# The first mixing written in two parts: weight conversions and one unit's scans beside the first channel products, the rest of three attention units beside what follows

## The chip, the cores and the metric

The program runs on one core of a Trainium2 chip. The metric is device time in microseconds (us) of one execution, from three runs of the kernel before: 521.94, 522.8 and 524.35, so a median of 522.8. A trace of another execution is shown below; its own time was 521.84 us.

## The reference

Two blocks follow each other. The first is a linear attention with a decaying state, for 4 batches, 8 heads, 768 positions and 48 features a head:

```
for t in range(S):
    cur = einsum('bhd,bhe->bhde', u * k[t], v[t])
    y[t] = einsum('bhd,bhde->bhe', r[t], state + cur)
    state = w[t][..., None] * state + einsum('bhd,bhe->bhde', k[t], v[t])
```

Its output, reshaped to x of 768 positions by 384 features a batch, goes into a mixer:

```
h = relu(x.T @ w_tok1) @ w_tok2        # tokens: 768 -> 256 -> 768
u = x + h.T
out = u + relu(u @ w_ch1) @ w_ch2      # channels: 384 -> 1536 -> 384
```

All of it is float32. The four mixer weights come in as 64-bit floats and are turned into float32 on the chip.

## The kernel before, in words

Attention is cut into 12 units: three for each of the four batches, each of 256 positions (two pieces of 128) and all 8 heads. `unit(i)` (L346) gives the steps of one unit as small functions:

- `ends` (L367): a backward scan of the decays on VectorE (L372), with a memset and a reciprocal. `keys` (L375) multiplies k by it (L377). `begins` (L379) is a forward scan (L380), `queries` (L382) multiplies r by that (L383).
- `tokens` and `copied`: TensorE transposes of the scaled keys into two PSUM banks (L287), ScalarE copies (L288).
- `own_u` (L385, ScalarE), `own_gram` (L390, TensorE) and `own_put` (L393, VectorE): the diagonal term with u. Units 0 to 3 make it this way; later units take it from an extra array `near` by VectorE (`products`, L397, and `sums_put`, L408).
- `gram` (L418) and `mask` (L421): products within a chunk of 64 positions and their masking.
- `carry` (L427): the outer products of keys and values. Then the chain over the four chunks of a unit: `update` (L440, VectorE, L448) adds to the state, `scaled` (L433, ScalarE, four small L438) scales it for the next chunk. Each `scaled` needs the `update` before it and each `update` the `scaled` before it.
- `before` (L450, TensorE L317): queries times the scaled states, so it needs the last `scaled`. `after` (L458, L338) adds the products within chunks, and `taken` (L462) copies the result into x.
- `ranges` (L361): two ScalarE passes (L364) that only flag decays out of range.

The mixing of a batch takes its x: `hidden` (L519) and `back` (L526) are the token part, `turn` (L533) transposes, then for each third of 256 positions come the channel products. In the first batch they are `up` (L540: six L545 matmul records for one of 12 column groups, then a ScalarE relu, L547) and `down` (L615: L621, twelve column groups summed in a PSUM bank, then a VectorE addition L625 and a store). The third third of the first batch uses `quarters` (L628, L639 and L643).

A weight is converted in pieces by `convert` (L195). A conversion loads one megabyte (two SP-queue transfers, L206) and runs on VectorE L209, L215, L221, L224 and twice L227, with L212 and L218 on ScalarE between L209 and L224. Two raw buffers alternate. Nine conversions, numbered 0 to 8 here, make up w_ch1 and w_ch2: 0 to 3 and half of 4 are w_ch1, the rest w_ch2. Conversions 0 and 1 are done before the channel products begin.

The order of the instructions on TensorE, VectorE and ScalarE is written out by hand: `strict` (L88) keeps each engine in the order in which the pieces are emitted. `woven` (L46) merges lists in proportion to costs given by hand: each piece has a cost, and pieces of two lists are sorted by the middle of their share of their list. Transfers on the SP queue are placed by the tile framework from the same order.

In the first batch (L820 to L828) three things are merged: the channel products of batch 0 (`ups`, `downs`), conversions 2 to 8, and all the steps of units 3, 4 and 5, which are batch 1's attention. `steps(i)` (L705) lists the steps of a unit, L828 weaves the three lists of steps over the whole stage. PSUM gives this stage six banks of one pool, which channel products, transposes and attention products share, and two banks for the outer products. Each later batch has its own order (`middle_mixing`, L800, and `last_mixing`, L778).

Of the kernel before, what the change touches and what calls it, by code (L numbers as in the profile page):

```python
# [24 lines left out]
UB = C // UC  # L25
# [20 lines left out]
def woven(*lists):  # L46

    keyed = []
    for n, pieces in enumerate(lists):
        total, at = sum(c for c, _ in pieces), 0.0  # L50
        for i, (c, f) in enumerate(pieces):
            keyed.append(((at + c / 2) / total, n, i, c, f))
            at += c
    return [(c, f) for *_, c, f in sorted(keyed, key=lambda e: e[:3])]
# [8 lines left out]
def rwkv6_then_mixer(  # L63
# [18 lines left out]
    pe, dve, act, pool, sp = nc.tensor, nc.vector, nc.scalar, nc.gpsimd, nc.sync  # L82
# [5 lines left out]
    def strict(*fs):  # L88

        for f in fs:  # L90
            done = len(block.instructions)
            f()
            for ins in block.instructions[done:]:
                if ins.engine in in_turn:
                    if in_turn[ins.engine]:
                        tc.add_manual_dep(ins, in_turn[ins.engine], no_sync, reason="order of issue")
                    in_turn[ins.engine] = ins.name
# [20 lines left out]
    u_rows = const.tile([128, DM], f32, name="u_rows")  # L118
# [10 lines left out]
    def load_w(i):  # L129
        if i < NU:  # L130
            for cols in (slice(MID, WCOLS), slice(0, MID)) if i == 0 else (slice(0, WCOLS),):
                sp.dma_start(ws[i % 2][:, cols], w[i][:, cols])

    def rk_of(i):
        return rks[i if i < UB else (i - UB) % 2]

    def load_rk(i):
        if i < NU:
            for n in (1, 0):
                for rows in (slice(0, 128),) if i < 3 else (slice(0, D), slice(P, P + D)):  # L140
                    sp.dma_start(rk_of(i)[rows, ts(n, COLS)], rk[i, n, rows, :])
# [3 lines left out]
    def load_v(i):  # L145
        if i < NU:
            vs[i] = vpool.tile([128, UC, DM], f32, name="vt")
            b, j = divmod(i, UB)
            sp.dma_start(vs[i], v[b, ts(j, UC * 128), :].rearrange("(c p) e -> p c e", p=128))

    def load_near(i):
        if UB < i < NU:
            nears[i] = apool.tile([128, UC, 2, DM], f32, name="near", bufs=1)
            sp.dma_start(nears[i], near[i - UB - 1])
# [82 lines left out]
    def conversion(*weights, rooms):  # L237
        pieces = [e for w in weights for e in blocks(*w)]
        return [convert(pieces[2 * n:2 * n + 2], *rooms(n)) for n in range(len(pieces) // 2)]
# [243 lines left out]
    def weight_sums(n):  # L483
        t1, t2, t4 = w_sums
        to, a, b = ((t1, w12, w11), (t2, w22, t1), (t4, w21, t2), (w12, w22, w12))[n]
        dve.tensor_sub(to, a, b)
# [11 lines left out]
    def less(to, a, b):  # L498
        dve.scalar_tensor_tensor(to, a, -1.0, b, op0=ALU.mult, op1=ALU.subtract)

    def left_sums():
        a = by_three
        return [lambda: dve.tensor_sub(A9, a(0, 1), a(1, 0)), lambda: dve.tensor_sub(A8, a(1, 0), a(1, 1)),
                lambda: dve.tensor_add(A0, a(1, 2), a(2, 1)), lambda: dve.tensor_add(A0, A0, A8), lambda: dve.tensor_sub(A8, A0, a(2, 1)),
                lambda: dve.tensor_sub(A7, a(0, 1), a(0, 0)), lambda: dve.tensor_sub(A12, a(2, 0), a(0, 2)),
                lambda: dve.tensor_add(A12, A12, A7), lambda: less(A11, A12, a(2, 2)), lambda: less(A7, A12, a(0, 2))]

    def lefts_in_place():
        a = by_three
        return [lambda: dve.tensor_sub(s_, A12, a(2, 0)), lambda: dve.tensor_sub(A2, A0, a(1, 2)),  # L510
                lambda: dve.tensor_sub(A10, a(1, 2), A9), lambda: dve.tensor_sub(A6, a(2, 2), A0), lambda: dve.tensor_sub(A13, a(0, 2), A9)]
# [190 lines left out]
    def mixing_of(bt):  # L702
        return mixing(bt, lambda: xs[bt], lambda n: out[bt, ts(n, 128), :])

    def steps(i):  # L705

        e = unit(i)
        up, by = e["updates"], e["scaled"]
        by_tokens = i > UB
        sums = e["products"] if by_tokens else [lambda: None] * 3  # L710
        some = lambda fs, c: [(c, f) for f in fs]
        return [(0.1, lambda: (i > UB and load_rk(i + 1), load_v(i + 1))), *([] if by_tokens else some(e["own_u"], 0.2)),
                (2.4, e["ends"]), (1.2, e["keys"]), (0.4, e["ranges"][0]), (2.2, e["begins"]), (1.0, e["tokens"]), (0.2, e["copied"][0]),
                *([] if by_tokens else [(1.0, e["own_gram"]), (1.3, e["own_put"]), (0.1, lambda: sp.dma_start(u_rows, u_all))]), (0.2, e["copied"][1]), (1.2, e["queries"]), (0.3, by[0]),
                (1.0, sums[0]), (1.0, e["carry"]), (1.0, sums[1]),
                (0.7, up[0]), (0.3, by[1]), (1.4, e["gram"]), (1.0, sums[2]), (0.1, lambda: load_near(i + 1)),
                (0.7, up[1]), (0.3, by[2]), (1.2, e["mask"]), (0.7, up[2]), (0.3, by[3]),
                *([(1.3, e["sums_put"])] if by_tokens else []), (0.7, up[3]),
                (0.1, lambda: load_w(i + 2)), (1.0, e["before"]), (0.1, e["seen"]), (1.5, e["ranges"][1]), (1.0, e["after"]), *some(e["taken"], 0.3)]
# [15 lines left out]
    hiddens, turned, ups, downs = mixing_of(0)  # L735
    h = [f for pair in zip(*hiddens) for _, f in pair]
    to_tok = conversion((wtok1, w_tok1, 2, 256), (wtok2, w_tok2, 2, 256), rooms=lambda n: (n % 2, n % 2))
    to_ch = conversion((wch1, w_ch1, 1, 512), (wch2, w_ch2, 4, 128), rooms=lambda n: (n % 2, 0) if n else (2, 1))
# [5 lines left out]
    e0, e1, e2 = (unit(i) for i in range(UB))  # L744
# [19 lines left out]
    def single(steps, n):  # L764
        return [(0.1, f) for f in (steps[5:] if n == 0 else steps[n < 3:])]
# [34 lines left out]
    def middle_mixing(bt):  # L800
        hiddens, turned, rights, thirds, quarters = mixing_of(bt)
        n = (bt + 1) * UB
        (a0, a1, a2), (b0, b1, b2), (c0, c1, c2) = (parts_of(i) for i in range(n, n + UB))
        *turned, end = turned
        of, sums = rights(0)
        hiddens = [e for h in hiddens for e in h]
        if bt == 1:
            a1[-5:-5] = products_of(n)
        pieces = woven(hiddens + turned[:6] + sums[:3] + turned[6:8] + sums[3:6] + turned[8:10] + sums[6:] + turned[10:], a0 + a1 + a2 + b0)
        for s, (att, near) in enumerate(((b1, n + 1), (b2 + c0, n + 2), (c1 + c2, n + 3))):  # L810
            ups = thirds(s, of)
            if s == 0:
                ups.insert(2, (0.01, end[1]))
            of, sums = rights(s + 1) if s < 2 else (None, [])
            pieces += ups[:1] + woven(ups[1:11], products_of(near) + sums[:2]) + ups[11:] + woven(att, woven(quarters(s), sums[2:]) if s < 2 else quarters(s))
        return pieces

    for bt in range(B):
        ahead = []
        if bt == 0:  # L820
            to_ch = [single(e, n) for n, e in enumerate(to_ch)]
            both = [f for e in zip(ups[0], ups[1]) for f in e]
            ahead = woven(turned, sum(to_ch[:2], []), [(1.3, e1["ranges"][1])])
            of_weights = [(0.1, lambda n=n: weight_sums(n)) for n in range(4)]
            both = woven(both[:6], [(1.3, f) for f in e2["ranges"]]) + both[6:]
            pieces = woven(both, sum(to_ch[2:8], [])) + woven(downs[0][:6], to_ch[8]) + downs[0][6:] + downs[1][:4]
            pieces += woven(downs[1][4:] + ups[2], of_weights + [(0.1, f) for f in left_sums()]) + woven(downs[2], [(0.1, f) for f in lefts_in_place()])
            pieces = woven([e for i in range(UB, 2 * UB) for e in steps(i)], pieces)  # L828
        elif bt < B - 1:
            pieces = middle_mixing(bt)  # L830
        else:
            pieces = last_mixing()
        strict(*(f for _, f in ahead + pieces))
# [113 lines left out]
```

## Time and profile before

| | |
|---|---|
| median of three runs | 522.8 us (521.94 to 524.35) |
| the profiled execution, its own time | 521.84 us |
| its span, first to last instruction | 520.1 us |
| TensorE, VectorE, ScalarE busy | 95%, 75%, 44% of the span |
| mean granted TensorE clock | 0.984 |

The first batch's channel products start at 63.71 us of the span and the token products of batch 1 (L522) at 179.66 us. By stages, with the busy time of each engine:

| stretch of the span, us | what | TensorE | VectorE | ScalarE | granted clock |
|---|---|---|---|---|---|
| 53.67 to 63.71 | `back` and `turn` of batch 0 | 9.51 | 7.76 | 6.86 | 1.00 |
| 63.71 to 79.90 | first channel products | 13.13 | 15.86 | 12.09 | 0.89 |
| 79.90 to 119.90 | up products, first down products | 39.84 | 33.66 | 25.35 | 1.00 |
| 119.90 to 179.66 | rest of batch 0 | 59.76 | 41.74 | 19.58 | 1.00 |
| 179.66 to 520.10 | batches 1 to 3 | 334.83 | 240.58 | 129.03 | 1.00 |

A float32 matmul shows as two records, so that one `up` group has six. The ends of matmuls are modelled, so a busy TensorE may be waiting inside; the distance from one start to the next tells more. Instructions on VectorE and ScalarE overlap the next one by about 0.1 us, and here too starts are compared.

### The profile page before, as it was taken

To read this page: it belongs to the slowest core of one execution; us is meant where nothing else is said; L and a number is where in the kernel's file an instruction comes from. 1 tells how busy PE (TensorE), PEld (TensorE's weight loads), DVE (VectorE), ACT (ScalarE), POOL (GpSimd) and SP (SyncE) were. 2 spreads that over 40 slices of the span, in tenths; PEclk is the share of its full clock that TensorE was granted. 3 is DMA by queue.
4 is the path that set the end of the run, shared out by engine and by line. 5 is a ranking of instruction groups with operands and counts; after the bars stand their busy time and mean duration, and the time that the engine had idled before them with its cause. 6 is when DMAs were issued, how large, how long until landed. Compare 5 with 4: busy or idle time off the path is not lost.

```text
span 520.1 us, 13317 instructions
## 1 busy us (share of the span) xinstructions
PE 492.2 (95%) x5794; PEld 429.4 (83%) x5794; DVE 388.1 (75%) x633; ACT 229.7 (44%) x533; POOL 1.3 (0%) x10
## 2 busy tenths in 40 slices
PE   3589979999999999999999999999999999999996
PEld 3476568866689868999999867999999859999996
DVE  7999798786596878987869668986858615684653
ACT  3868785671243236524335436524435414531300
POOL 0000000000000000000000000000000000000000
PEclk9779989999999999999999999999999999999999
DMA  8887448523314333122211432100000000000000
GB/s 305 320 262 208 135 145 279 168 89 115 104 38 133 92 112 84 62 69 66 63 62 62 142 96 63 61 18 15 3 32 1 18 15 1 1 2 33 0 33 33
DMA packets 20945, 46.06 MB, mean 89 GB/s; under 512 B 2128, under 2 KB 13008, under 8 KB 20880
## 3 DMA queue, kind: packets, MB, share of 16 engines
q1 hardware_dynamic: 20736, 45.14, 27.2%
q8 instruction: 47, 0.77, 0.6%
q14 instruction: 18, 0.15, 0.1%
q10 hardware_dynamic: 144, 0.00, 0.0%
HBM read 40.41 MB, written 4.72 MB: 87 GB/s over the span
## 4 chain that ended last, share of the span: by engine, by line
PE 76%; DVE 15%; ACT 5%; issue 3%; DMA 1%; DVEq 0%
PE z_ps L582 18%; PE q_ps L643 12%; PE q_ps L639 12%; PE z_ps L545 8%; PE h_ps L529 6%; PE h_ps L522 6%; PE h_ps L621 4%; PE gram L257 2%; PE y_ps L317 2%; PE y_ps L338 2%; DVE w L380 2%; PE xT_ps L537 2%; DVE z L590 2%; DVE to_end L372 1%; DVE rk L383 1%
## 5 line engine op out<-in xcount | busy, mean ns | idle before, releaser
L438 ACT ACTIVATE before<-state,to_end 112x48 f32<-112x48 f32 x176 | 44.4, 324 | 60.0 <-DVE state L448 56.5
L587 ACT COPY z<-z_ps 128x512 f32<-128x512 f32 x54 | 30.6, 587 | 57.4 <-PE z_ps L582 39.5
L590 DVE TENSOR_TENSOR z<-z,z_ps 128x512 f32<-128x512 f32 x54 | 35.9, 682 | 24.6 <-PE z_ps L582 15.9
L545 PE MATMUL z_ps<-xT,wch 128*128 128x256 f32 x216 | 50.1, 387 | 0.0
L599 ACT ACTIVATE z<-z 128x512 f32<-128x512 f32 x54 | 33.3, 631 | 33.1 <-DVE z L590 29.0
L545 PEld LDWEIGHTS z_ps<-xT,wch 128*128 128x128 f32 x216 | 40.8, 193 | 6.2 <-DVE wch L227 0.3
L639 PE MATMUL q_ps<-wch,z 128*128 128x192 f32 x222 | 42.9, 329 | 0.2
L643 PE MATMUL q_ps<-wch,z 128*128 128x192 f32 x222 | 43.0, 330 | 0.0
L639 PEld LDWEIGHTS q_ps<-wch,z 128*128 128x128 f32 x222 | 36.4, 190 | 0.9 <-ACT z L599 0.6
L643 PEld LDWEIGHTS q_ps<-wch,z 128*128 128x128 f32 x222 | 36.7, 190 | 0.5
L529 PE MATMUL h_ps<-h,wtok 128*128 128x384 f32 x96 | 35.1, 492 | 0.6 <-ACT h L524 0.6
L593 DVE TENSOR_TENSOR z<-z,z_ps 128x512 f32<-128x512 f32 x45 | 30.0, 683 | 7.0 <-PE z_ps L582 6.5
L522 PE MATMUL h_ps<-x,wtok 128*128 128x384 f32 x96 | 32.9, 490 | 0.0
L531 DVE TENSOR_TENSOR x<-x,h_ps 128x384 f32<-128x384 f32 x24 | 13.2, 552 | 26.2 <-PE h_ps L529 26.2
L621 PE MATMUL h_ps<-wch,z 128*128 128x384 f32 x96 | 32.4, 490 | 0.2 <-DVE wch L227 0.2
L582 PE MATMUL z_ps<-rk,wch 128*128 128x128 f32 x256 | 31.2, 275 | 0.0
L582 PEld LDWEIGHTS z_ps<-rk,wch 128*128 128x128 f32 x256 | 30.0, 192 | 0.0
L372 DVE TENSOR_TENSOR_SCAN to_end<-w,starts 112x1041 f32<-112x1041 f32 (+1 forms) x13 | 28.1, 2160 | 2.1 <-DMA w<-in_w_dram 1.7
L380 DVE TENSOR_TENSOR_SCAN w<-w,starts 112x1041 f32<-112x1041 f32 x12 | 27.8, 2320 | 0.0
L643 PE MATMUL q_ps<-scratch,z 128*128 128x192 f32 x144 | 27.9, 330 | 0.0
L621 PEld LDWEIGHTS h_ps<-wch,z 128*128 128x128 f32 x96 | 17.8, 190 | 11.6 <-DVE wch L227 0.3
L639 PE MATMUL q_ps<-scratch,z 128*128 128x192 f32 x144 | 27.3, 326 | 0.0
(181 smaller groups left out, 916.2 us busy)
## 6 DMA issues: line engine op xcount, KB each, us to landing
rk<-in_rk_dram SPq DMA_DIRECT2D x36, 192.0 KB, 3.8
near<-in_near_dram SPq DMA_DIRECT2D x8, 768.0 KB, 4.6
w<-in_w_dram SPq DMA_DIRECT2D x11, 520.5 KB, 4.7
vt<-in_v_dram SPq DMA_DIRECT2D x12, 384.0 KB, 3.7
out_dram<-o SPq DMA_DIRECT2D x24, 192.0 KB, 1.9
spare<-in_w_ch_dram SPq DMA_DIRECT2D x8, 512.0 KB, 4.5
scratch<-in_w_ch_dram SPq DMA_DIRECT2D x8, 512.0 KB, 5.2
rk<-in_rk_dram SPq DMA_DIRECT2D x6, 512.0 KB, 8.5
```

The source lines that it names most:

```text
L372: dve.tensor_tensor_scan(to, of, start, 0.0, op0=ALU.mult, op1=ALU.add)
L380: dve.tensor_tensor_scan(w_[:ROWS], w_[:ROWS], starts[:ROWS], 0.0, op0=ALU.mult, op1=ALU.add)
L438: act.mul(t[:ROWS, a], state[bt, g][:ROWS, a], by_last(c, j)[:, a:a + 1])
L522: pe.matmul(sums[i], wtok1[:, c, ts(i, 128)], x_of()[:, c, :], start=(c == 0), stop=(c == C - 1))
L529: pe.matmul(ps, wtok2[:, i, ts(c, 128)], h1[:, i, :], start=(i == 0), stop=(i == DTOK // 128 - 1))
L545: pe.matmul(ps, wch1[:, m, ts(jt, 128)], xT[:, m, ts(s, SEG)], start=(m == 0), stop=(m == DM // 128 - 1))
L582: pe.matmul(ps[:, q], lefts[r][:, ts(q, 128)], of[r], start=first and q == 0, stop=end and q == JB - 1, skip_group_check=True)
L590: dve.tensor_add(to(n), to(n), ps)
L599: act.activation(to(n), to(n), AF.Relu)
L621: pe.matmul(ps, zs[s][:, jt, ts(n, 128)], wch2[:, jt, :], start=(jt == 0), stop=(jt == NJ - 1))
L639: pe.matmul(L["q"], a[:, j, :], b[:, j, :], start=(j == 0), stop=False)
L643: pe.matmul(L["q"], a[:, j, :], b[:, j, :], start=False, stop=(j == HJ - 1))
```

## The change

`steps(i)` returns a unit in two lists, `first` (scans and what prepares the keys) and `second`. Unit 3's `first` is woven with conversions 2 to 8, all 24 `up` groups of the first two thirds and the first four `down` pieces. The rest of unit 3, all of units 4 and 5, and unit 2's two range flags are woven with the remaining products. Within unit 3, `own_gram`, `own_put`, the load of `u_rows`, the first range flag and `queries` move from between the scans into the second list. No instruction is added or removed, and the arithmetic stays.

```
@@ steps(i), at the end @@
-        return [(0.1, lambda: (i > UB and load_rk(i + 1), load_v(i + 1))), *([] if by_tokens else some(e["own_u"], 0.2)),
-                (2.4, e["ends"]), (1.2, e["keys"]), (0.4, e["ranges"][0]), (2.2, e["begins"]), (1.0, e["tokens"]), (0.2, e["copied"][0]),
-                *([] if by_tokens else [(1.0, e["own_gram"]), (1.3, e["own_put"]), (0.1, lambda: sp.dma_start(u_rows, u_all))]), (0.2, e["copied"][1]), (1.2, e["queries"]), (0.3, by[0]),
+        loads, ranges, copied = (0.1, lambda: (i > UB and load_rk(i + 1), load_v(i + 1))), (0.4, e["ranges"][0]), some(e["copied"], 0.2)
+        ends, keys, begins, tokens, queries = ((c, e[n]) for c, n in ((2.4, "ends"), (1.2, "keys"), (2.2, "begins"), (1.0, "tokens"), (1.2, "queries")))
+        if by_tokens:
+            first = [loads, ends, keys, ranges, begins, tokens, *copied, queries]
+        else:
+            first = [loads, *some(e["own_u"], 0.2), ends, keys, begins, tokens, *copied]
+        second = [] if by_tokens else [(1.0, e["own_gram"]), (1.3, e["own_put"]), (0.1, lambda: sp.dma_start(u_rows, u_all)), ranges, queries]
+        return first, [*second, (0.3, by[0]),
                 (1.0, sums[0]), (1.0, e["carry"]), (1.0, sums[1]),
...
@@ the order of batch 0 @@
-            both = woven(both[:6], [(1.3, f) for f in e2["ranges"]]) + both[6:]
-            pieces = woven(both, sum(to_ch[2:8], [])) + woven(downs[0][:6], to_ch[8]) + downs[0][6:] + downs[1][:4]
-            pieces += woven(downs[1][4:] + ups[2], of_weights + [(0.1, f) for f in left_sums()]) + woven(downs[2], [(0.1, f) for f in lefts_in_place()])
-            pieces = woven([e for i in range(UB, 2 * UB) for e in steps(i)], pieces)
+            (first, second), *rest = (steps(i) for i in range(UB, 2 * UB))
+            pieces = woven(first, woven(both, sum(to_ch[2:8], [])) + woven(downs[0][:4], to_ch[8]))
+            mixed = downs[0][4:] + downs[1][:4] + woven(downs[1][4:] + ups[2], of_weights + [(0.1, f) for f in left_sums()])
+            mixed += woven(downs[2], [(0.1, f) for f in lefts_in_place()])
+            pieces += woven([(0.4, f) for f in e2["ranges"]] + second + sum((a + b for a, b in rest), []), mixed)
```

## The prediction

> **What bounds the kernel now.** First the page's busy shares and clock row, then stage windows, then TensorE's timeline of the stage that the change reorders.
>
> ```profile
> PE 492.2 (95%) x5794; PEld 429.4 (83%) x5794; DVE 388.1 (75%) x633; ACT 229.7 (44%) x533; POOL 1.3 (0%) x10
> ...
> PEclk9779989999999999999999999999999999999999
> ```
> ```profile
> 63.71:79.90 16.19, 13.13 (x116) 10.94 (x115) 15.86 (x21) 12.09 (x22) 0.00 (x0) 0.89 0.44 135
> ...
> 119.90:179.66 59.76, 59.76 (x660) 47.12 (x661) 41.74 (x60) 19.58 (x59) 0.00 (x0) 1.00 0.30 91
> 179.66:520.10 340.44, 334.83 (x3558) 306.10 (x3556) 240.58 (x430) 129.03 (x295) 0.00 (x0) 1.00 0.15 45
> ```
>
> TensorE is the bound. From 63.71 us on it lacks work only in 63.71 to 79.90 (13.13 of 16.19 us busy, clock 0.89) and at the very end. The columns after the length are TensorE, weight loads, VectorE, ScalarE, GpSimd, then clock. Now the hole itself, on the timeline of TensorE and VectorE, and the clock in a window of 2 us:
>
> ```profile
> 63.71 6.82 PE L545 MATMUL z_ps<-xT,wch 128*128 128x256 f32 x30
> ...
> 72.27 1.22 DVE L377 TENSOR_TENSOR rk<-rk,to_end 112x1024 f32<-112x1024 f32 x1
> ...
> 73.59 1.94 PE L287 MATMUL k_ps<-ident,rk 128*128 128x128 f32 x8 [3.06 <-issue]
> ...
> 75.32 2.24 PE L545 MATMUL z_ps<-xT,wch 128*128 128x256 f32 x6
> ...
> 77.50 1.16 PE L257 MATMUL gram<-rk,near 48*64 48x64 f32 x64
> ```
> ```profile
> 74.00:76.00 2.00, 2.00 (x10) 0.50 0.39 138
> ```
>
> After five `up` groups TensorE reaches unit 3's transposes, whose keys (L377) VectorE writes only until 73.5. The trace calls the wait "issue"; the transposes read what L377 writes, so it is the keys. Thirty records at 0.2167 us end at 70.21, so 3.3 us are lost to 73.59. Then the clock reads 0.50: the eight transposes take 1.73 us to the next start (0.90 at 112.44), and six L545 take 2.18 against 1.30 plus 0.18 of switching. That adds 0.8 and 0.7. With 0.3 us of small waits (states at 98.18, a weight at 119.90), 5.1 us of this stage are recoverable.
>
> [...]
>
> **The change, first part.** 24 groups at 1.30 us come before any attention on TensorE, so the 3.3 + 1.5 us hole goes: the transposes stand behind them and one `down` piece, at 63.71 + 31.2 + 1.3 = 96.2, and the keys are long done. What can be late instead is the weights. On VectorE seven conversions and unit 3's scans must pass. The price of a conversion comes from these rows of the timeline, VectorE's and ScalarE's:
>
> ```profile
> 81.09 0.68 DVE L209 TENSOR_SCALAR scratch<-scratch 128x1024 uint16<-128x1024 uint16 x1
> ...
> 83.43 1.22 DVE L221 SCALAR_TENSOR_TENSOR scratch<-scratch 128x1024 f32<-128x1024 uint32 x1
> 85.53 0.69 DVE L224 TENSOR_TENSOR scratch<-scratch 128x1024 bf16<-128x1024 bf16 x1 [0.89 <-ACT scratch L218]
> 86.26 1.29 DVE L227 SCALAR_TENSOR_TENSOR wch<-scratch 128x512 f32<-128x512 f32 x2
> ```
> ```profile
> 84.07 0.39 ACT L547 ACTIVATE z<-z_ps 128x256 f32<-128x256 f32 x1 [0.41 <-PE z_ps L545]
> 84.35 1.15 ACT L218 ACTIVATE scratch<-scratch 128x1024 bf16<-128x1024 int32 x1
> ...
> 112.86 1.15 ACT L212 ACTIVATE scratch<-scratch,rebias 128x1024 uint16<-128x1024 uint16 x1 [2.41 <-DVE scratch L209]
> ```
>
> VectorE alone needs 0.60 + 0.60 + 1.15 + 0.72 + 1.21 = 4.3. But L224 waits for ScalarE: from L209's start 0.71 to L212, 1.06, a relu 0.28, L218 1.13, 0.03 = 3.21. Then 0.72 + 1.21: 5.14 a conversion, unless other VectorE work fills the gap. In the new order conversion 2 starts at 65.12 as before; four `own_u` (0.46 each) stand in ScalarE's queue before its L218, which starts at 69.13; it is done at 72.2. Conversion 3: 77.4. `ends` 2.64 (66.37 to 69.01): 80.0. Conversion 4: 85.1. Conversion 5 holds the keys (1.14): 90.5. Conversion 6 holds `begins` (2.24): 97.1. Conversion 7: half at 101.7, all at 102.2. Conversion 8 has a keys' copy (0.47) for a relu: 107.6.
>
> TensorE needs conversion 2 at 74.1 (72.2: covered), 4's first half at 85.4 (84.6: covered by 0.8), 7's first half at the fifth `down` piece, 101.1: 96.2 + 0.9 transposes + 0.1 + three pieces at 1.29. That is **0.55 us late**. Conversion 8 is due at 109.4 and covered. Bank waits are covered: a group waits for the relu six groups earlier, which is done 2.5 us or more ahead (group 17: relu 11 at 82, due 84.5).
>
> Loads: the SP queue now issues conversions 3 to 8 in a row; `near` for unit 4 (768 KB, 4.6 us), `u_rows` and the decays of unit 5 come behind them. A raw buffer is loaded when L221 and L218 two conversions earlier are done: the last at 93.8, landing 5.2 us later at 99, needed at 102.2. `near` is needed at 131. No load becomes late.
>
> **Second part.** Units 3 to 5 now share the 71 us after the transposes. The change puts a smaller distance between each unit's first state and its `before`. Queued behind VectorE's two L625, which wait for the end of the first third's `down` sums, are unit 3's `update` 1 and mask. From the later sum, at E (115.3 by TensorE's count: dense pieces 1.29, attention steps 1.09, 0.18 a switch): L625 0.6, mask 1.2, `update` 0.3, then four L438 at 0.23, one a pair of heads. The first of these scaled states is there at E + 2.4; `before` arrives at E + 2.6 and uses them in turn: no stall. Unit 4: its last `scaled` at 142.1, `before` at 143.3: none. Unit 5: from the end of `quarters`' third product (L643), VectorE does L661 0.37, L405 0.87, L687 0.87, `update` 0.27, a weight sum 0.6, mask 1.2, L665 0.47, L687 0.87, `update` 0.27: 5.8 us, so scaled states come at 6.1 to 6.8. TensorE has five half products of 0.98 and half of `before`, 5.4 us, ahead of them. Paced by them it ends **about 1.0 us late**. Behind `before` wait only Q7's end and `after`; the batch-1 token products begin with older positions of x.
>
> Moves without cost: the flags L364 (1.15 each) go behind copies that ScalarE has free time for (19.58 of 59.76 us). Number of switches between dense and attention matmuls: 16 before and after. POOL has nothing here.
>
> **Sum.** 5.1 recovered - 0.55 - 1.0 = 3.55, taken as 3.5 us. All later stages are TensorE-bound and ordered as before; L681 on VectorE waits for TensorE's last product there in both, so they shift whole. The profiled execution would go from 521.84 (span 520.1 plus 1.74) to 518.3. The median of the runs is 0.96 above it: **519.3 us**.
>
> Unknown is how well VectorE keeps the walk's pace. Below: VectorE's bare 4.3 per conversion would make conversion 7 over 3 us earlier, stall zero. Above: before, L209 of conversion 2 to the end of 8 took 54.6 us, some 17 of them attention, so 5.37 a conversion, 0.23 more than mine; over five 1.2 us. I take 5.14, whose terms the order gives.
>
> **Rivals.**
> *Whole gain*: VectorE on time twice (L224 finds ScalarE done, unit 5's masks run in gaps): 522.8 - 5.1 = 517.7. For it: `before` takes its states one by one. Against: seven L224 need two ScalarE passes each.
> *Half gain*: conversions at 5.37, weights 0.55 + 1.2 = 1.75 us late, unit 5 1.0, and 1 us more in the chains of units 3 and 4: 5.1 - 3.75 = 1.35 gained, 521.4. For it, from the waits between 60 and 200 us (total, times, longest):
>
> ```profile
> ACT before L438 <- DVE state L448: 19.0, 8, 5.4
> ...
> DVE scratch L224 <- ACT scratch L218: 5.2, 4, 3.0
> ```
> The longest wait of L224 was 3.0 us, at 90.3, when ScalarE's L218 stood behind a relu that waited for TensorE.
> *Slower*: the same FIFO catch at the fifth `down` piece. If two of conversions 3 to 7 lose 3.0 us where I have 0.8, conversion 7 is 4.4 later, TensorE stands 5 us, the clock halves (1.5 as above), unit 5 costs 1.0: 7.5 - 5.1 = 2.4 lost, 525.2. [...] Against: in the walk every relu ahead of an L212 or L218 is over 0.5 us done.
> *The change doesn't do it*: the keys' wait simply returns; excluded, since transposes follow all `up` groups.
>
> **Chances.** Mine (2.6 to 4.5 gained) 0.48, whole gain 0.17, half gain (under 2.6 either way) 0.25, slower 0.10. 0.5% is 2.6 us, about what a measurement can tell. Faster 0.65, same 0.25, slower 0.10. Range: from the whole gain with 0.7 us of spread, 517.0, to the half-gain case losing 0.9, 523.7.
>
> **What would show it.** Right: L545 144 records in a row from 63.7 to 95, clock 1.0 there, L287 at 96 without wait; a hole of 0.5 to 1 us in L621 near 101 ended by L227; a wait of 1 us in L317 near 169; L522 of batch 1 at about 176 instead of 179.66. Wrong: L224 waiting over 1 us several times, holes over 3 us, a clock below 1 after 63 us, or a new wait after L522.

## The result and the profile after

| | before | after |
|---|---|---|
| median | 523.31 us (20 runs, 520.34 to 525.53) | 519.68 us (20 runs, 518.40 to 524.95) |
| ratio, 95% interval | | 0.9948 (0.9925 to 0.9970) |
| the profiled execution, its own time | 521.84 us | 522.58 us |
| its span | 520.1 us | 520.9 us |
| first L545 to the first L522 of batch 1 | 63.71 to 179.66: 115.95 us | 67.78 to 180.32: 112.54 us |

The change makes the kernel 0.5% faster, and 0.8% in a second comparison (0.9924, 0.9902 to 0.9946). The kernel before compared with itself, in four runs below, gave ratios from 0.9985 to 1.0032, so 0.5% is not far above what such a comparison resolves. The profiled execution of after is nevertheless the longer of the two. So the first thing to do is to cut the span at points that both traces have: the opening (up to the first L545), the stage that was reordered (up to batch 1's first L522), and the rest. The stage lost 3.41 us, the opening, whose order on the engines is the same in both, was 4.07 us longer in this execution, and the rest differs by 0.1 us. The page of after, and its stage windows (the columns are those of the windows before: TensorE, weight loads, VectorE, ScalarE, GpSimd, clock, DMA share, GB/s):

```profile
PE 493.1 (95%) x5794; PEld 430.1 (83%) x5794; DVE 388.8 (75%) x633; ACT 229.3 (44%) x533; POOL 1.3 (0%) x10
...
PEclk9788999999999999999999999999999999999999
```
```profile
67.78:83.97 16.19, 16.19 (x77) 14.01 (x76) 12.97 (x19) 9.58 (x19) 0.00 (x0) 1.00 0.61 194
...
123.97:180.32 56.35, 55.74 (x773) 45.53 (x771) 47.41 (x64) 24.27 (x72) 0.00 (x0) 1.00 0.37 108
180.32:520.90 340.58, 334.84 (x3557) 306.09 (x3556) 240.71 (x430) 129.51 (x296) 0.00 (x0) 1.00 0.15 45
```

The first 16.19 us of channel products had 13.13 us of busy TensorE at clock 0.89 before; now they are full, at clock 1.00. The clock row's 8s, in the third and fourth of 13 us slices, lie in the opening. Now TensorE's timeline in the stage (start, length, engine, line, operation, records, idle time before and what ended it):

```profile
67.78 31.43 PE L545 MATMUL z_ps<-xT,wch 128*128 128x256 f32 x144
...
100.34 1.04 PE L287 MATMUL k_ps<-ident,rk 128*128 128x128 f32 x8
...
105.61 1.56 PE L621 MATMUL h_ps<-wch,z 128*128 128x384 f32 x4 [0.36 <-DVE wch L227]
...
173.69 0.79 PE L317 MATMUL y_ps<-before,rk 48*64 48x48 f32 x36
175.09 0.99 PE L317 MATMUL y_ps<-before,rk 48*64 48x48 f32 x28 [0.61 <-ACT before L438]
176.01 1.24 PE L643 MATMUL q_ps<-wch,z 128*128 128x192 f32 x6
```

The 144 L545 records run without a break, and the transposes find their keys. Two new waits stand in the stage: the fifth `down` piece for its weights (L227), and unit 5's `before` for its scaled states (L438). From L317's start to the next product are 2.32 us; unit 3's and unit 4's, without a wait, take 1.08. On VectorE, the conversion that the fifth piece waits for (timeline), and the two waits shown of before (total us, times, longest, between 60 and 200 us):

```profile
102.26 1.23 DVE L221 SCALAR_TENSOR_TENSOR scratch<-spare,scratch 128x1024 f32<-128x1024 uint32 x1
104.14 0.69 DVE L224 TENSOR_TENSOR scratch<-scratch 128x1024 bf16<-128x1024 bf16 x1 [0.65 <-ACT scratch L218]
104.86 1.30 DVE L227 SCALAR_TENSOR_TENSOR wch<-scratch 128x512 f32<-128x512 f32 x2
```
```profile
ACT before L438 <- DVE state L448: 23.6, 8, 5.8
...
DVE scratch L224 <- ACT scratch L218: 5.1, 5, 2.3
```

From L221's start to L224's are 1.88 us, 1.15 of them L221's own: 0.73 us of waiting for ScalarE's second pass, where the walk had 0.86. No conversion waits 3 us; the one wait of L224 over 1 us, 2.3 us, is conversion 2's behind the four `own_u`, which the walk had.

### The profile page after: what moved, and what is told of

Read it like the earlier page. It is cut to its first block, busy times and chain, and to the rows that moved or that the text cites. A ratio compares the mean times of both kernels' runs of the same rounds, so it can differ in the third digit from the quotient of the medians.

```text
span 520.9 us, 13323 instructions
## 1 busy us (share of the span) xinstructions
PE 493.1 (95%) x5794; PEld 430.1 (83%) x5794; DVE 388.8 (75%) x633; ACT 229.3 (44%) x533; POOL 1.3 (0%) x10
## 4 chain that ended last, share of the span: by engine, by line
PE 72%; DVE 16%; ACT 5%; issue 3%; DMA 2%; SPq 0%; DVEq 0%; ACTq 0%
PE z_ps L582 18%; PE q_ps L643 12%; PE q_ps L639 11%; PE h_ps L529 5%; PE h_ps L621 5%; PE h_ps L522 5%; PE z_ps L545 3%; PE y_ps L317 3%; PE gram L257 2%; PE y_ps L338 2%; DVE w L380 2%; PE kv_ps L303 2%; PE xT_ps L537 2%; DVE z L590 2%; DVE to_end L372 1%
## 5 line engine op out<-in xcount | busy, mean ns | idle before, releaser
L438 ACT ACTIVATE before<-state,to_end 112x48 f32<-112x48 f32 x176 | 44.4, 324 | 65.2 <-DVE state L448 61.5
L545 PE MATMUL z_ps<-xT,wch 128*128 128x256 f32 x216 | 48.1, 381 | 0.0
L545 PEld LDWEIGHTS z_ps<-xT,wch 128*128 128x128 f32 x216 | 40.6, 190 | 6.0 <-DVE wch L227 0.3
L643 PE MATMUL q_ps<-wch,z 128*128 128x192 f32 x222 | 43.3, 331 | 0.0
L639 PE MATMUL q_ps<-wch,z 128*128 128x192 f32 x222 | 42.8, 329 | 0.2
L639 PEld LDWEIGHTS q_ps<-wch,z 128*128 128x128 f32 x222 | 36.5, 190 | 0.9 <-ACT z L599 0.6
L643 PEld LDWEIGHTS q_ps<-wch,z 128*128 128x128 f32 x222 | 36.5, 190 | 0.6
L621 PE MATMUL h_ps<-wch,z 128*128 128x384 f32 x96 | 33.3, 494 | 0.4 <-DVE wch L227 0.4
L522 PE MATMUL h_ps<-x,wtok 128*128 128x384 f32 x96 | 33.3, 495 | 0.0
L643 PE MATMUL q_ps<-scratch,z 128*128 128x192 f32 x144 | 27.7, 329 | 0.0
L639 PE MATMUL q_ps<-scratch,z 128*128 128x192 f32 x144 | 27.4, 327 | 0.0
L582 PE MATMUL z_ps<-xT,wch 128*128 128x128 f32 x216 | 27.1, 275 | 0.0
```

Source lines behind the costliest of these rows:

```text
L438: act.mul(t[:ROWS, a], state[bt, g][:ROWS, a], by_last(c, j)[:, a:a + 1])
L522: pe.matmul(sums[i], wtok1[:, c, ts(i, 128)], x_of()[:, c, :], start=(c == 0), stop=(c == C - 1))
L545: pe.matmul(ps, wch1[:, m, ts(jt, 128)], xT[:, m, ts(s, SEG)], start=(m == 0), stop=(m == DM // 128 - 1))
L582: pe.matmul(ps[:, q], lefts[r][:, ts(q, 128)], of[r], start=first and q == 0, stop=end and q == JB - 1, skip_group_check=True)
L621: pe.matmul(ps, zs[s][:, jt, ts(n, 128)], wch2[:, jt, :], start=(jt == 0), stop=(jt == NJ - 1))
L639: pe.matmul(L["q"], a[:, j, :], b[:, j, :], start=(j == 0), stop=False)
```

## The experiments

Fourteen executions of eight different programs were profiled. Each is cut the same way; the last column is the execution's own time less opening and stage.

| profile | own time | opening | stage | rest |
|---|---|---|---|---|
| before | 521.84 | 63.71 | 115.95 | 342.18 |
| before_again | 525.24 | 68.67 | 114.36 | 342.21 |
| before_third | 521.72 | 63.73 | 115.80 | 342.19 |
| before_fourth | 522.58 | 64.40 | 116.00 | 342.18 |
| before_fifth | 522.74 | 64.60 | 115.95 | 342.19 |
| before_sixth | 523.55 | 65.31 | 116.03 | 342.21 |
| after | 522.58 | 67.78 | 112.54 | 342.26 |
| after_again | 519.25 | 64.49 | 112.56 | 342.20 |
| keys_one_later | 519.82 | 63.67 | 113.85 | 342.30 |
| keys_three_later | 519.65 | 64.20 | 113.26 | 342.19 |
| scan_behind | 517.60 | 63.55 | 111.89 | 342.16 |
| unit5_earlier | 517.29 | 63.74 | 111.33 | 342.22 |
| both_mended | 518.04 | 65.18 | 110.66 | 342.20 |
| weights_late | 526.80 | 65.23 | 119.29 | 342.28 |

All variation between the executions of one kernel is in the opening and, before the change, in the stage. The stage is therefore the measure below.

### Both kernels once more

> The kernel before, unchanged, profiled once more. The stage from the first record of L545 to batch 1's first L522 took 115.95 us in the first profile. If the opening's 63.71 us there against 67.78 us after is a difference between executions of one code, this profile shows an opening anywhere between 63 and 68 us and the same stage within 0.5 us. If the change lengthens the opening, it stays near 63.7 us.

> The kernel after, unchanged, profiled once more. My theory: the stage takes 112.5 us again within 0.5 us, with a hole near 0.4 us in L621 and 1.2 us lost at unit 5's L317; the opening, whose code is the same, lies anywhere between 63 and 68 us, and the median of the times is 3 to 4 us under the kernel before. Rival: the change lengthens the opening by other reads from memory; then it is near 67.8 us again.

Medians 522.19 us (before_again, 14 runs), 518.76 us (after_again, 21 runs), 523.02 us (before beside them, 50 runs). After's stage is the same to 0.02 us, with 0.39 us of idle time in L621. The medians stand 4.26 us apart, a little more than expected. After's opening is 64.49 us, before's now 68.67, just over the range that I gave: the change does not lengthen the opening, which differs between executions of one code. But before's stage was 114.36 us, 1.59 less than in the first profile and not within the 0.5 us that I expected. Timelines of TensorE at unit 3's transposes, in before_again and, for comparison, in before_third:

```profile
78.56 1.06 PE L287 MATMUL k_ps<-ident,rk 128*128 128x128 f32 x8 [3.07 <-issue]
79.46 1.46 PE L545 MATMUL z_ps<-xT,wch 128*128 128x256 f32 x6
```
```profile
73.62 1.94 PE L287 MATMUL k_ps<-ident,rk 128*128 128x128 f32 x8 [3.07 <-issue]
75.35 2.08 PE L545 MATMUL z_ps<-xT,wch 128*128 128x256 f32 x6
```

The idle time is the same, 3.07 us; the slow rows behind it are missing in before_again, and they are the difference. So hole and half clock are two losses, and the second need not follow the first.

The granted clock shows it too. In before it changes at 18.87, 29.11, 32.52, 35.94, 73.48 and 76.90 us, in after at 19.55, 29.79, 43.44 and 46.85 us; in each of the two traces these times lie multiples of 3.41 us apart. Two windows of before around 73.48 us, then two of before_again that share the hole between them:

```profile
70.07:73.48 3.41, 0.46 (x3) 0.06 (x1) 3.22 (x6) 2.17 (x6) 0.00 (x0) 1.00 0.63 169
73.48:76.90 3.42, 3.31 (x12) 3.07 (x13) 3.42 (x5) 2.77 (x4) 0.00 (x0) 0.50 0.39 138
```
```profile
73.83:77.24 3.41, 1.66 (x8) 1.13 (x6) 3.20 (x5) 3.40 (x8) 0.00 (x0) 1.00 0.25 37
77.24:80.66 3.42, 2.10 (x14) 1.89 (x14) 3.42 (x5) 1.56 (x2) 0.00 (x0) 1.00 0.72 270
```

In before 2.95 us of the hole lie in the 3.41 us ahead of 73.48 us, and the next 3.42 us have clock 0.50. In before_again 1.75 and 1.32 us of the hole lie in the two windows, and the clock is 1.00 in both. What decides between the two cases is not shown.

To see how often the half clock comes, and where the longer executions of before lose their time, the kernel before was profiled four times more:

> The kernel before, unchanged, a third profile. In the ten profiles so far the time less the opening (to the first L545) less the stage (to batch 1's first L522) is 342.2 us within 0.1 us. The medians of before and after stand 4.3 us apart on one chip, but the stages only 1.8 us (before_again) or 3.4 us (before). Theory: what is missing is lost at half clock behind the hole, and in an execution of 522 us or more the stage is 116 us or longer. Rival: the opening is longer in the kernel before, 65 us or more, with a stage of 114.4 to 116.0 us.

> The kernel before, unchanged, a fourth profile; theory and rival as for the third: a stage of 116 us or longer in an execution of 522 us or more, or an opening of 65 us or more with a stage of 114.4 to 116.0 us.

> The kernel before, unchanged, a fifth profile; theory and rival as for the third and fourth.

> The kernel before, unchanged, a sixth profile. Four of five had a stage of 115.8 to 116.0 us and one of 114.4 us; the executions of 524 us and more, of which one alone has been profiled (opening 68.67 us, stage 114.36 us), are what is still unexplained. If this one is above 524 us: theory, its opening is 66 us or longer with a stage of 114.4 to 116.0 us; rival, its stage is 117 us or longer. Below 523 us: the stage is 115.8 to 116.0 us with the slow rows, or 114.4 us without.

All four stages are 115.80 to 116.03 us, so the slow rows came in five of six profiles. In these four the mean clock from 72 to 82 us is 0.83, as in before; in before_again it is 1.00.

For an execution of 522 us or more I had expected a stage of 116 us or longer, or else an opening of 65 us or more. before_fourth and before_fifth (522.58 and 522.74 us) have stages of 116.00 and 115.95 us and openings of 64.40 and 64.60 us. The time of before_sixth, 523.55 us, fell between the cases that I had set out for it; its stage is 116.03 and its opening 65.31 us. From before_third to before_sixth the time grows by 1.83 us, the stage by 0.23 and the opening by 1.58. So longer executions had a longer opening, not a longer stage. With a median opening of 64.5 us (six profiles) and a stage of 115.95, before comes to 522.65 us, within its medians of 521.95 to 523.83.

Before has a long tail of slower executions: 524 us or more were 5 of 20 in the first comparison and 14 of 50 in the second. For after the same lateness begins 3.4 us lower, because its stage is shorter by that: 520.6 us or more were 8 of 20 and 1 of 21. So the kernel after has such executions too, and their share differs from comparison to comparison. Only one such execution of before was profiled, before_again, and its opening was long; the cause stays open.

### Half of the lateness taken away, in the kernel before

```
+            moved[:] = [(1.0, e["tokens"]), (0.2, e["copied"][0]), (0.2, e["copied"][1])]
...
+            pieces = [e for e in pieces if e not in moved]
+            at = [f for _, f in pieces].index(groups[6 - 1]) + 1
+            pieces[at:at] = moved
```

> The kernel before with unit 3's transposes and both copies of its keys behind the sixth group of L545 instead of the fifth: 1.3 us later, where the keys were 3.3 us late. My theory counts 1.5 us of the 5.1 us as half clock that the hole brings on: a hole of 2.0 us is left, and if that is too short to halve the clock the transposes take 0.9 us and the six groups 1.48 us each again, and the stage takes 115.95 - 1.3 - 1.5 = 113.1 us. Rival: the slow rows behind the hole have another cause than its length; then they stay slow and the stage takes 115.95 - 1.3 = 114.6 us.

The stage took 113.85 us. TensorE's timeline:

```profile
73.56 1.07 PE L287 MATMUL k_ps<-ident,rk 128*128 128x128 f32 x8 [1.77 <-issue]
...
75.65 1.56 PE L545 MATMUL z_ps<-xT,wch 128*128 128x256 f32 x6
77.75 4.15 PE L545 MATMUL z_ps<-xT,wch 128*128 128x256 f32 x18 [0.54 <-ACT z L547]
```

Of the hole 1.77 us are left, 1.30 less than 3.07, which is as far as the transposes were moved: it was the wait for the keys. Nothing behind it is slow (the clock is 1.00 from 73.6 to 81 us), so the clock's part went too in this one profile. That the hole is now too short to halve the clock is not shown: behind the 3.07 us of before_again it stayed at 1.00 too. The 0.75 us by which 113.1 is missed are mostly a wait that I had not named, of an `up` group for a relu. The median is 519.82 us (5 runs; ratio to before 0.9958, 0.9921 to 0.9995).

### The whole lateness taken away, in the kernel before

The same edit with `groups[8 - 1]`.

> The kernel before with one move: unit 3's transposes (L287 there) and both copies of its keys go behind the eighth group of L545 instead of the fifth, that is 3 x 1.3 = 3.9 us later, past the 3.3 us by which the keys were late. Nothing else is moved. My theory, that the whole gain is this wait and the half clock behind it: the wait at the transposes and the half-clock rows go, nothing new is late (unit 5's conversion and sums stay where they were), and the stage takes 115.95 - 5.1 = 110.9 us, some 1.6 us less than after; the time is 517 to 518.5 us. Rival, that the two-part order itself is what gains and the lateness only moves to the next consumer of unit 3's scan: a hole of 2 us or more appears at L621 or at unit 3's L317, and the stage stays above 114 us.

519.57 us (22 runs; ratio to before 0.9944, 0.9925 to 0.9962), stage 113.26 us: faster than before, but neither the 110.9 of the theory nor the 114 of the rival. This one move gives 2.69 of the change's 3.41 us. TensorE and ScalarE at the transposes:

```profile
76.04 0.60 PE L287 MATMUL k_ps<-ident,rk 128*128 128x128 f32 x4
78.26 0.66 PE L287 MATMUL k_ps<-ident,rk 128*128 128x128 f32 x4 [1.62 <-ACT z L547]
```
```profile
74.62 1.15 ACT L212 ACTIVATE scratch<-scratch,rebias 128x1024 uint16<-128x1024 uint16 x1 [1.87 <-DVE scratch L209]
...
76.82 1.11 ACT L218 ACTIVATE scratch<-spare 128x1024 bf16<-128x1024 int32 x1
77.83 0.92 ACT L547 ACTIVATE z<-z_ps 128x256 f32<-128x256 f32 x3
```

The first four transposes no longer wait for the keys. The second four need a PSUM bank that `up` group 6 still holds. Its relu stands in ScalarE's queue behind L212 and L218 of conversion 3 and a range flag between them (L364, 1.15 us), and L212 waited 1.87 us for VectorE's L209, which stands behind the keys' product. So the late VectorE reaches TensorE by another way: 1.62 us here, and 0.4 us more in unit 3's L317 at 95.66. The attention products among the `up` groups take banks of the same six, so a relu is due earlier than where `up` groups alone go round. In the kernel after they do, and the 144 records show no wait. The keys' wait was not the only thing that the two-part order removed. This chain is read from the trace; no run took it apart.

### The two new waits, one at a time and together

scan_behind, after with unit 3's `begins` put behind the conversions:

```
-            first = [loads, *some(e["own_u"], 0.2), ends, keys, begins, tokens, *copied]
+            first = [loads, *some(e["own_u"], 0.2), ends, keys, (2.2, lambda: None), tokens, *copied]
-        second = [] if by_tokens else [(1.0, e["own_gram"]), (1.3, e["own_put"]), (0.1, lambda: sp.dma_start(u_rows, u_all)), ranges, queries]
+        second = [] if by_tokens else [(1.0, e["own_gram"]), (1.3, e["own_put"]), (0.1, lambda: sp.dma_start(u_rows, u_all)), ranges, (0.01, e["begins"]), queries]
```

> The kernel after with unit 3's begins (L380) taken out of the conversions and put ahead of its queries; the rest is as it was. My theory: conversion 7 is late only by what VectorE does for unit 3 ahead of it, so the 0.36 us wait of L621 for L227 goes, unit 3's and unit 4's L317 still wait for nothing, and the stage takes 112.5 - 0.4 = 112.1 us. Rival, that conversion 7 waits on ScalarE or on its load and not on VectorE's queue: the wait stays at 0.3 us or more.

unit5_earlier, after with work of VectorE taken from in front of unit 5's states:

```
-                (1.0, sums[0]), (1.0, e["carry"]), (1.0, sums[1]),
-                (0.7, up[0]), (0.3, by[1]), (1.4, e["gram"]), (1.0, sums[2]), (0.1, lambda: load_near(i + 1)),
+                (1.0, sums[0]), (1.0, e["carry"]), (1.0, sums[1]), *([(0.01, sums[2])] if i == UB + 2 else []),
+                (0.7, up[0]), (0.3, by[1]), (1.4, e["gram"]), (1.0, sums[2] if i != UB + 2 else lambda: None), (0.1, lambda: load_near(i + 1)),
...
-            mixed += woven(downs[2], [(0.1, f) for f in lefts_in_place()])
+            lips = [(0.1, f) for f in lefts_in_place()]
+            mixed += lips[:3] + woven(downs[2], lips[3:])
```

> The kernel after with unit 5's third sum (L405) put ahead of the first update and three of the in-place weight sums (L425) put ahead of the third group of L621. My theory: unit 5's L317 loses 1.24 us because VectorE has 1 us too much in its queue ahead of what makes before; with it out of the way the L317 of 28 records has no wait over 0.2 us, and the stage takes 112.5 - 1.2 = 111.3 us. Rival, that ScalarE (L438) is what is late there: the wait for L438 stays at 0.5 us or more.

The in-place weight sums run as L510 and L511 (L425, named in the forecast, is the mask), and the edit puts three of them ahead of the third third's products, L639 and L643. The two moves were not tried apart.

both_mended has both edits:

> The kernel after with its two losses mended: unit 3's first pieces of scan (begins, L380, 2.2 us by the planner's price) are taken out of the conversions and put ahead of its queries, and unit 5's third sum (L405) and three of the in-place weight sums (L425) are put where VectorE is early. TensorE's order is not changed. My theory: the 0.36 us hole in L621 and the 1.24 us at unit 5's L317 go, at most 0.2 us of either is left, and the stage takes 112.5 - 1.5 = 111.0 us; the time is 1.3 to 1.6 us under after. Rival, that these waits are only where a VectorE that is behind all through shows: they come back as waits of the same size at another unit's L317 or at batch 1's L522, and the stage stays at 112 us or more.

Stages: 111.89, 111.33 and 110.66 us, so 0.67, 1.23 and 1.90 us less than after_again. The medians of scan_behind and unit5_earlier, two runs each, are 517.83 and 517.26 us (ratios to before 0.9925 and 0.9914). The parts add up, and nothing came back elsewhere; scan_behind gives more than the 0.4 us that I read from the idle time, because the records behind the wait start slowly too (four L621 take 1.49 us to the next start, 1.29 without the wait). TensorE in both_mended, where the two waits were:

```profile
98.61 5.33 PE L621 MATMUL h_ps<-wch,z 128*128 128x384 f32 x16
...
170.46 1.15 PE L317 MATMUL y_ps<-before,rk 48*64 48x48 f32 x64
...
175.84 4.68 PE L522 MATMUL h_ps<-x,wtok 128*128 128x384 f32 x14
```

All sixteen L621 records and all 64 of L317 run in one piece. The time of both_mended is 516.80 us (6 runs; ratio to before 0.9873, 0.9836 to 0.9911), some 2 us under after's 518.76 on the same chip, where 1.3 to 1.6 were expected: a version that beats both kernels.

### The price of late weights

```
+        def again():
+            t = L["to_end"][:ROWS]
+            for n in range(4):
+                dve.tensor_tensor(t, t, t, op=ALU.max)
...
+            to_ch[7].insert(0, (0.0, delays[0]))
```

> The kernel after with four more passes of VectorE (112 x 1041, each 1.14 us by the row of L377) ahead of conversion 7, extra work that leaves the values as they are: the weights of the fifth group of L621 come 4.6 us later. It puts a price on the way in which the change could have ended slower, the first-in first-out walk of the weights. My theory: TensorE's hole in L621 grows from 0.36 to 5.0 us, the clock is halved after it as it was after the 3.3 us hole of before (some 1.5 us more), and the stage takes 112.5 + 4.6 + 1.5 = 118.6 us, over the 115.95 us of before. Rival without the clock: 117.1 us. Rival, that VectorE has slack ahead of conversion 7: less than 2 us are lost, and the stage stays under 114.5 us.

526.24 us (2 runs; ratio to before 1.0086, 1.0056 to 1.0116), stage 119.29 us. VectorE's extra work, then TensorE, then TensorE's clock between 106 and 110 us (below the added function, lines have numbers five higher here):

```profile
98.41 5.08 DVE L378 TENSOR_TENSOR to_end<-to_end 112x1041 f32<-112x1041 f32 x4
```
```profile
108.06 2.93 PE L626 MATMUL h_ps<-wch,z 128*128 128x384 f32 x4 [5.36 <-DVE wch L227]
110.91 1.55 PE L257 MATMUL gram<-rk,near 48*64 48x64 f32 x64
```
```profile
106.00:110.00 4.00, 1.95 (x3) 1.18 (x4) 3.35 (x6) 1.58 (x3) 0.00 (x0) 0.50 0.00 0
```

The extra passes hold VectorE for 4.99 us (98.41 to conversion 7's L209 at 103.40; I had planned 4.6), and the fifth piece starts 4.98 us later in the stage than in after_again (42.83 against 37.85 us from the first L545). VectorE has no slack ahead of conversion 7: what is put there goes to TensorE one for one. Behind the hole, at half clock, the four L621 take 2.85 us to the next start instead of 1.49, and the gram 1.48 instead of 1.09: 1.75 more. 4.98 + 1.75 = 6.73, the stage's growth over after_again. The clock is at 0.50 from 104.99 to 111.82 us: it fell inside the hole, when 2.29 us of it had passed.

## Why the prediction was right, point by point

**The whole.** 519.3 us was forecast, 519.68 measured, and 518.76 in the second comparison, both in the range. The forecast started from three runs with a median of 522.8 us, where 20 gave 523.31. The gain in the stage was to be 3.55 us; it is 115.95 - 112.54 = 3.41, and 3.24 to 3.49 with the other slow-row profiles of before. Against before_again's stage it is 1.8: in an execution without half clock the change is worth the hole less the two new waits. By time the gain is 0.52% in the first comparison and 0.76% in the second, so at the edge of what a measurement can tell.

**What can be recovered: 5.1 us.** 115.95 - 110.66 = 5.29 by the version without any of these waits. Its parts were 3.3 for the hole and 1.5 for the half clock behind it. The second is measured by before_again: 1.59. What I wrote as a sure consequence of the hole is only a frequent one: five of six, and that the profile I worked from was one of the five was luck. Where the half clock begins differs as well: with the transposes in before_third (the clock fell at 73.18 us; 1.73 us to the next start), and behind them in before_fifth (at 75.51 us; transposes 0.90 us to the next start, six L545 2.57). In weights_late it fell when 2.29 us of the hole had passed. In the opening of after, where the matmuls are smaller, it fell at 43.44 us, and of the 3.41 us ahead of that (40.03 to 43.44 us) 1.29 were idle by the records. What decides whether and when it falls is not shown.

**Conversion 7 0.55 us late.** 0.65: in after_again 6.78 us pass from the transposes to the gram (97.05 to 103.83), in scan_behind, without the wait, 6.13. The idle time by the records is only 0.39; I counted from start to start and so came nearer. The walk by 5.14 us a conversion held: moved by the opening's 4.07 us, conversions 4 to 8 were to start at 84.07, 89.17, 94.57, 101.17 and 106.27, and their L209 stand at 83.84, 88.92, 94.33, 100.94 and 106.08. Neither end of the bounds that I gave for it, 4.3 and 5.37, was taken.

**Units 3 and 4 without a stall, unit 5 1.0 us late.** Right in place; in size it is 1.23 to 1.25 (2.33 us to the next start instead of 1.08; 1.23 gained by unit5_earlier). The chain on VectorE took 5.74 us from the product's end (168.93 to 174.67) where 5.8 were counted. The term that was too small is what follows the wait: the 28 last records take 0.92 us, because they come at the pace of four L438 (their starts lie in four groups 0.22 us apart), instead of some 0.5. With the measured terms, 5.29 - 0.65 - 1.24 = 3.40, the measured gain. All three terms were taken too small, by 0.19, 0.10 and 0.24 us, and it is luck that these misses largely cancel.

**The rest.** L522 of batch 1 was forecast "at about 176"; it stands at 180.32 because the opening was 4.07 us longer, and at 177.05 in after_again, whose opening was 0.78 longer than before's. A clock below 1 "after 63 us" was my sign for wrong; the row of 8s in the page of after is such a slice, but of the opening. A place on the time axis of another execution was a poor sign; distances from a common point hold. The rest, forecast to shift whole, is 342.2 us in every profile.

**The rivals.** The whole gain failed for the two reasons given, but two moves on VectorE recover it (both_mended). Half gain did not come. The slower one is real in its mechanism, and was under-priced: I had 7.5 us lost for a hole of 5 us, weights_late shows 119.29 - 110.66 = 8.63 (hole and clock 6.73, and the 1.90 that after loses anyway). That costs 3.34 us against before's stage, where I had 2.4. The length of the hole alone does not decide whether the clock halves: with 3.05 to 3.07 us it halved in five profiles (mean 0.83 from 72 to 82 us) and stayed at 1.00 in before_again.

## What to carry to other kernels

Cut a trace at points that both kernels share before comparing times: an opening that varies by 5 us hid a gain of 3.4 here. Where a strict order is rewritten, walk each engine's queue with measured start distances, and give the places where the walk is late by half a microsecond their own experiment; both could be mended by moving a few VectorE instructions, with nothing else touched. And where one engine is late, moving its nearest consumer is not enough: ask which PSUM bank, and which copy behind it in ScalarE's queue, is late next.

## What the runs showed that I had not expected

The same 3.07 us of idle TensorE cost nothing more in one execution, and some 1.6 us of half clock in five others, so the kernel before has stages of 114.4 and of 116.0 us. No edit here set which of the two comes. The opening, with the same instructions in the same order, took between 63.55 and 68.67 us in fourteen profiles, while everything behind the stage stayed within 0.14 us (342.16 to 342.30). What sets the opening's length in an execution was not settled: the two longest ones have waits of 1.1 to 1.3 us between attention products and half-clock rows there (mean clock 0.93 from 40 to 64 us in both, 1.00 in before) that shorter ones lack in part, and no experiment took these apart.
